# Group 0's FFN is cut in two around group 1, with second products two units behind

## The chip, the cores and the metric

The kernel runs on one core of a Trainium2 chip. The core has TensorE (PE, with its weight loads listed as PEld), VectorE (DVE), ScalarE (ACT), GpSimd (POOL) and SyncE (SP, which here only issues DMAs); each works through its own instruction list in order. The metric is device time in microseconds (us), the median of three runs.

## The reference

A linear attention runs over 768 tokens for 4 batches of 8 heads, and its output (3072 tokens by 384) goes through a feed-forward net (FFN):

```python
for t in range(768):
    cur = einsum('bhd,bhe->bhde', u * k[t], v[t])
    y[t] = einsum('bhd,bhde->bhe', r[t], state + cur)
    state = w * state + einsum('bhd,bhe->bhde', k[t], v[t])
h = x @ w_in                              # [3072,384] @ [384,2048]
out = (h * clip(h + 3, 0, 6) / 6) @ w_out # [3072,2048] @ [2048,384]
```

## The kernel before

**Attention.** Tokens are cut into 12 chunks of 64, and each chunk into two halves (two batches each): 24 halves, numbered `i`. Four halves make a group of 512 tokens, and there are six groups (`NG`). A half needs five loads at most (`load`, L199), DVE or POOL products that build `ks`, `RP`, `X` and `KH` (`prepare`, `attention`), and one block of small matmuls on PE, here called its visit (`visit`): the visit of half i adds its keys and values to the state in bank `U` (`keep`), makes its outputs (`outputs`) and, from `APART` on, also the scores of half i+1. Then DVE builds the next `X` from the scores (`choose`), DVE scales `U` into `St`, ACT copies the output to `x` as its rounded part (L404), and DVE subtracts that to get the rest (L405). After every second half six small DMAs move rows of `x` to other partitions (L412, 16 partitions each). `x` has two buffers, by group parity.

**FFN.** A unit is one group by one of 16 slices of the hidden dimension (`NF`): 96 units. `ffn1` is nine 128x512 matmuls (L137) into one of two banks `h`; ACT applies the bias and lower clip (L430), DVE clips and multiplies (L432), ACT rounds into `g` (L436), DVE subtracts to get the rest (an L196 row `g<-t,g`). `ffn2` is nine matmuls (L144) from `g` (three buffers) that add to the three PSUM banks `o`. A key `"ffn"` that all of them write keeps these blocks in the order in which they are added. After a group's slice 15 the three sums are scaled by 1/6 into SBUF, two by ACT (L460) and one by DVE (L461), and leave by DMA (L462).

**Weights.** The 64-bit weights of a slice come as one 768 KB load into one of two buffers `raw` and are converted by `weights(f)` (L212): `z` by ACT or DVE (L223), `cv` by ACT (L225) and by DVE (L226), a shift and or on DVE (L228), an add (an L196 row `z<-z,cv`), the rounded part `w_hi` by ACT or DVE (L232, L233), and the rest `w_lo` on POOL only (L234, in the trace an L196 row `w_lo<-z,w_hi`).

**Order.** Nothing is issued as written. `Schedule.add` notes each operation's cost per engine and what it reads and writes; `order` lists them with a planner: an operation's rank is the longest chain of costs behind it, each engine takes the ready operation that can begin first (by rank among those that begin within 0.1), and one that two engines could do goes to the one that would end it first. `WAIT`, `ISSUE`, `FLIGHT` and `KB_US` are the planner's prices. Where its plan leaves PE idle, filler matmuls on `ident` are put (`warm`, L532).

The loop at L497 adds units group by group. While group 0's units are added, the slices 3 to 15 are converted, one for each unit, and the attention of the next group is added at every fourth slice: `if c0 == 0 and f % 4 == 0 and 4 + 4 * g + f // 4 < NHALF: attend(4 + 4 * g + f // 4)`. So halves 4 to 7 are spread over group 0's 16 units. `ffn2` is added one unit behind: `while len(pend) > (2 if ns == 1 else 1): ffn2(*pend.pop(0))` with `ns` always 2.

Of the kernel before, what the change touches and what calls it, by code (L numbers as in the profile page):

```python
# [23 lines left out]
NHALF = 2 * NSTEP  # L24
# [14 lines left out]
WAIT = {"pe": 0.26, "act": 0.13, "dve": 0.12, "pool": 0.12, "sp": 0.05}  # L39
ISSUE, FLIGHT, KB_US = 0.46, 1.95, 300.0  # L40
LEAD = 8.0
EARLY = 8
APART = 4


class Schedule:
# [3 lines left out]
    def __init__(self):  # L50
        self.ops, self.writer, self.readers = [], {}, {}

    def add(self, costs, reads, writes, emit, lead=0.0, port=False):

        n = len(self.ops)
        deps = set()
        for r in reads:
            if r in self.writer:
                deps.add(self.writer[r])
            self.readers.setdefault(r, []).append(n)  # L60
        for w in writes:
            if w in self.writer:
                deps.add(self.writer[w])
            deps.update(self.readers.pop(w, ()))
            self.writer[w] = n
        deps.discard(n)
        self.ops.append((costs, deps, emit, lead, {"pool", "dve"} if port else {"pool"}))
        return n

    def order(self):  # L70
# [7 lines left out]
        for i in reversed(range(n)):  # L78
            costs = ops[i][0]
            w = max(WAIT[e] for e in costs)  # L80
            own = FLIGHT + costs["sp"] / KB_US if "sp" in costs else min(costs.values())
            rest[i] = own + max((rest[j] + w for j in succ[i]), default=0.0)
            rest[i] = max(rest[i], 0.0)
        prio = [rest[i] + ops[i][3] for i in range(n)]
        waits = [len(ops[i][1]) for i in range(n)]
        at = [dict.fromkeys(ops[i][0], 0.0) for i in range(n)]
        free = dict.fromkeys(WAIT, 0.0)
        port = line = 0.0
# [6 lines left out]
        while ready:  # L95
            best = None
            for e in free:
                here = [i for i in ready if e in ops[i][0]]
                if not here:
                    continue  # L100
                t = min(begin(i, e) for i in here) + 0.1
                for i in sorted((i for i in here if begin(i, e) <= t), key=lambda i: -prio[i]):
                    start = begin(i, e)
                    end = start + (ISSUE if e == "sp" else ops[i][0][e])
                    if any(begin(i, x) + c < end for x, c in ops[i][0].items() if x != e):
                        continue
                    if best is None or start < best[0]:
                        best = (start, e, i)
                    break
            start, e, i = best  # L110
            ready.remove(i)
            if e == "sp":
                free[e] = start + ISSUE
                line = ready_at = max(line, start + FLIGHT) + ops[i][0][e] / KB_US
            else:
                free[e] = ready_at = start + ops[i][0][e]
            if e in ops[i][4]:
                port = free[e]
            done.append((start, free[e], e, i))
            for j in succ[i]:  # L120
                for x in at[j]:
                    at[j][x] = max(at[j][x], ready_at + (WAIT[e] if x != e or e == "sp" else 0.03))
                waits[j] -= 1
                if not waits[j]:
                    ready.append(j)
# [14 lines left out]

def project(nc, o, w_hi, w_lo, f, g, clear, ms=range(3)):
    for m in ms:
        for k, (wl, hl) in enumerate(PARTS):
            nc.tensor.matmul(o[m], (w_hi, w_lo)[wl][:, f, 1, 128 * m:128 * m + 128], g(hl),  # L144
                             start=(clear and k == 0), stop=(f == NF - 1 and k == 2), skip_group_check=True)


def fast_path(tc, mp, pp, sb, w_hi, w_lo, b3, wm, badi, hps, ops3, rT, kT, rt, kt, vt, wp, wu, wcat, out):
# [26 lines left out]
    mask = one("mask", [128, C], U8)  # L175
    KH, ks = two("KH", [128, 8, D]), two("ks", [112, 8, C])
    NW = 2 * DM
    raw, z = two("raw", [128, NW], I64), two("z", [128, NW])
# [21 lines left out]
    def load(i):  # L200
        q = i % 2
        for name, dst, src, cost in (("kT", kTt, kT, 224), ("rT", rTt, rT, 224), ("V", V, vt, 192),
                                     ("kt", ktt, kt, 192), ("rt", rtt, rt, 192)):
            if name == "rt" and i < EARLY:
                continue
            S.add({"sp": cost}, [], [(name, q)], lambda e, dst=dst, src=src: dma(dst[q], src[i]), LEAD)
# [5 lines left out]
    def weights(f):  # L212
        S.add({"sp": 768}, [], [("raw", f % 2)], lambda e: dma(raw[f % 2], wcat[f]))
        words = "p (n two) -> p n two"
# [18 lines left out]
              else dve.tensor_copy(hi, zf), port=True)  # L233
        tensor_tensor(0.87, 1.9, [kz, ("wh", f)], [("wl", f)], lo, zf, hi.bitcast(F32), ALU.subtract, "p")  # L234


    def consts():
# [26 lines left out]

        S.add({"sp": 7}, [], ["wpt"], lambda e: dma(wpt, wp), 400)

# [109 lines left out]
    def attention(i):  # L376
# [19 lines left out]
        if going:  # L396
            S.add({"dve": 0.47}, ["U", "E"], [("St", q)], lambda e: dve.tensor_tensor(
                out=St[q], in0=U[0:112], in1=PQ[:, :, C:C + 1].broadcast_to([112, 8, D]), op=ALU.mult), LEAD)
        x = xt[g % 2]
        cs = slice(128 * hf, 128 * hf + 128)  # L400
        yt = y_[0:112].rearrange("e (p b) t -> e p b t", b=2)
        hi, lo = (x[0:112, c, :, hl, cs].rearrange("e p (b t) -> e p b t", t=C) for hl in range(2))
        kx = ("x", g % 2, c, hf)
        S.add({"act": 0.49}, [ky], [kx + (0,)], lambda e: act.copy(out=hi, in_=yt), LEAD)  # L404
        S.add({"dve": 0.60}, [ky, kx + (0,)], [kx + (1,)], lambda e: dve.tensor_tensor(  # L405
            out=lo, in0=yt, in1=hi.bitcast(F32), op=ALU.subtract), LEAD)
        if hf == 1:
            for n in range(2):
                for j in range(3):
                    r0, d0 = 64 * n + 16 * j, 64 * n + 48  # L410
                    S.add({"sp": 32}, [("x", g % 2, c, b, hl) for b in range(2) for hl in range(2)],
                          [("xh", g % 2, c, n, j)], lambda e, j=j, r0=r0, d0=d0: dma(  # L412
                              x[d0:d0 + 16, c, j].bitcast(F32), x[r0:r0 + 16, c, 3].bitcast(F32)), LEAD)
# [3 lines left out]
    def ffn1(n, g, f, c0, ns):  # L417
        x, h, t, gt = xt[g % 2], hps[n % 2], tt[n % 2], gg[n % 3]
        T = 256 * ns
# [5 lines left out]
        for c in range(c0, c0 + ns):  # L425
            reads += [("x", g % 2, c, hf, hl) for hf in range(2) for hl in range(2)]
            reads += [("xh", g % 2, c, k, j) for k in range(2) for j in range(3)]
        first = S.add({"pe": 1.03 * ns}, reads, [("h", n % 2), "ffn"], emit)
# [14 lines left out]
    def ffn2(n, g, f, c0, ns, ms=range(3)):  # L443
        T = 256 * ns
        gt = gg[n % 3]
        cols = slice(256 * c0, 256 * c0 + T)

        def emit(e):

            project(nc, [o[:, cols] for o in ops], w_hi, w_lo, f, lambda hl: gt[:, hl, :T],  # L450
                    f == 0 and c0 == 0, ms)
        S.add({"pe": 1.03 / 3 * ns * len(ms)}, [("g", n % 3, 0), ("g", n % 3, 1), ("wh", f), ("wl", f)],
              [f"o{m}" for m in ms] + ["ffn"], emit)
        if f == NF - 1:
            t0 = 512 * g + 256 * c0
            for m in ms:
                o, kb = stage[3 * c0 + m]
                o = o[:, :T]
                S.add({"act": 0.1 + 0.2 * ns} if m != 1 else {"dve": 0.05 + 0.28 * ns}, [f"o{m}"], [kb],
                      lambda e, m=m, o=o: act.mul(out=o, in_=ops[m][:, cols], mul=1.0 / 6.0) if e == "act"  # L460
                      else dve.tensor_scalar(out=o, in0=ops[m][:, cols], scalar1=1.0 / 6.0, scalar2=None, op0=ALU.mult))  # L461
                S.add({"sp": 128 * ns}, [kb], [], lambda e, m=m, o=o: dma(  # L462
                    out[128 * m:128 * m + 128, t0:t0 + T], o))

    def flag():

        wf = KH[0].rearrange("p h d -> p (h d)")[0:1]
        S.add({"sp": 2}, [], [("KH", 0)], lambda e: dma(wf, wu[0:1]))

# [11 lines left out]
    load(0)  # L481
    S.add({"sp": 192}, [], ["ubt"], lambda e: [dma(
        ubt[TOK[n]].rearrange("p h d -> p (h d)"), wu[2 + n:3 + n].broadcast_to([64, DM])) for n in range(2)])
# [5 lines left out]

    units = [(g, f, 0, 2) for g in range(NG) for f in range(NF)]  # L490
    pend, held = [], []
    for i in range(4):
        attend(i)
    for f in range(3):
        weights(f)
    nw = 3
    for n, u in enumerate(units):  # L497
        g, f, c0, ns = u
        if g == 0 and c0 == 0 and nw < NF:
            weights(nw)  # L500
            nw += 1
        if c0 == 0 and f % 4 == 0 and 4 + 4 * g + f // 4 < NHALF:
            attend(4 + 4 * g + f // 4)
        if g == NG - 2 and f == NF - 1:
            flag()
        ffn1(n, *u)
        pend.append((n,) + u)
        while len(pend) > (2 if ns == 1 else 1):
            ffn2(*pend.pop(0))
# [31 lines left out]
def rwkv_ffn_kernel(ctx: ExitStack, tc: tile.TileContext, rT, kT, rt, kt, vt, wp, wu, wcat, ys, out):  # L541
# [21 lines left out]
    with tc.If(bad != 0):  # L563
        with tc.tile_pool(name="fb", bufs=1) as fb, tc.tile_pool(name="fl", bufs=1) as fl:
# [45 lines left out]
            with tc.For_i(0, NG, 1) as g:  # L610
# [9 lines left out]
                for f in range(NF):  # L620
# [6 lines left out]
                    nc.vector.tensor_tensor(out=gt[:, 1], in0=t, in1=gt[:, 0].bitcast(F32), op=ALU.subtract)  # L627
                    project(nc, ops, w_hi, w_lo, f, lambda hl: gt[:, hl], f == 0)
                for m in range(3):
# [65 lines left out]
```

## Time and profile before

| what | value |
|---|---|
| median of three runs | 520.24 us (518.41 to 520.96) |
| the profiled execution, its own time | 523.83 us |
| its span, first to last instruction | 521.9 us |
| PE busy | 496.1 us, 95% |
| DVE busy | 302.6 us, 58% |
| ACT, POOL busy | 189.5 us (36%), 66.4 us (13%) |

The profiled execution is 3.59 us (0.7%) above the median, and 1.93 us of its time lie outside the span. Busy shares are of the whole span; matmuls are pipelined, so a busy PE may still be waiting a little or running at its lower clock. In the forty-slice view each digit is a share in tenths, 9 being 90% or more.

### The profile page before, as it was taken

How to read it: one execution, taken by the hardware profiler on the slowest of the kernel's cores; microseconds unless marked ns; L12 is line 12 of the kernel's file. 1: busy time of each engine (PE TensorE's matmuls, PEld its weight loads, DVE VectorE, ACT ScalarE, POOL GpSimd, SP SyncE). 2: the span in 40 equal slices, each digit the busy share in tenths (PEclk: the TensorE clock that was granted, in tenths of full speed). 3: DMA queues.
4: the chain of work that ended last, by engine and by line, in shares of the span. 5: the costliest groups of instructions: out<-in, count | busy, mean ns of one | idle time of the engine just before them, and what ended most of it. 6: DMA issues, size and time to landing. Idle time of an engine off the chain costs nothing.

```text
span 521.9 us, 11782 instructions
## 1 busy us (share of the span) xinstructions
PE 496.1 (95%) x5126; PEld 407.5 (78%) x5126; DVE 302.6 (58%) x469; ACT 189.5 (36%) x292; POOL 66.4 (13%) x52
## 2 busy tenths in 40 slices
PE   8868999898999999999999999999999999999994
PEld 7767787787778888778888778888788888788882
DVE  8776788887983359633379633389433372333331
ACT  2413767354333343233333333333433332333331
POOL 1411333211300011100012100023000020000000
PEclk9797999797999999999999999999999999999998
DMA  8874344553250016410026310035200010100001
GB/s 274 240 224 134 123 138 164 163 182 104 75 161 0 1 53 171 135 60 2 0 82 184 93 62 0 0 109 164 93 9 0 1 47 19 60 1 0 0 1 66
DMA packets 22908, 44.29 MB, mean 85 GB/s; under 512 B 3649, under 2 KB 11970, under 8 KB 22850
## 3 DMA queue, kind: packets, MB, share of 16 engines
q1 hardware_dynamic: 22850, 43.47, 27.3%
q8 instruction: 42, 0.69, 0.6%
q14 instruction: 16, 0.13, 0.1%
HBM read 36.38 MB, written 4.72 MB: 79 GB/s over the span
## 4 chain that ended last, share of the span: by engine, by line
PE 72%; DVE 13%; ACT 4%; issue 4%; DMA 3%; SPq 3%; POOL 0%; ACTq 0%; DVEq 0%; POOLq 0%
PE h L137 30%; PE o L144 29%; PE h L532 4%; PE Y L295 3%; PE SC L295 3%; DVE g L196 2%; SPq L412 2%; DMA kt<-kt 2%; DVE t L432 2%; DVE KH L196 1%; DMA rt<-rt 1%; PE U L295 1%; DVE x L405 1%; DVE rt L196 1%; PE o L295 1%
## 5 line engine op out<-in xcount | busy, mean ns | idle before, releaser
L144 PE MATMUL o<-g,w_hi 128*128 128x512 f32 x576 | 199.5, 400 | 3.7 <-DVE g L196 1.5
L137 PE MATMUL h<-x,w_hi 128*128 128x512 f32 x576 | 165.4, 396 | 0.0
L432 DVE SCALAR_TENSOR_TENSOR t<-t,h 128x512 f32<-128x512 f32 x96 | 65.8, 685 | 127.4 <-ACT t L430 127.4
L144 PEld LDWEIGHTS o<-g,w_hi 128*128 128x128 f32 x576 | 108.4, 189 | 33.3 <-DVE g L196 4.1
L430 ACT ACTIVATE t<-h,b 128x512 f32<-128x512 f32 x96 | 66.1, 688 | 174.4 <-PE h L137 174.2
L137 PEld LDWEIGHTS h<-x,w_hi 128*128 128x128 f32 x576 | 108.7, 190 | 23.8
L144 PE MATMUL o<-g,w_lo 128*128 128x512 f32 x288 | 113.5, 394 | 0.0
L196 DVE TENSOR_TENSOR g<-t,g 128x512 fp32r<-128x512 f32 x96 | 70.3, 732 | 45.3 <-ACT g L436 45.3
L436 ACT CAST g<-t 128x512 fp32r<-128x512 f32 x96 | 59.6, 620 | 86.7 <-DVE t L432 86.6
L137 PE MATMUL h<-x,w_lo 128*128 128x512 f32 x288 | 82.5, 395 | 0.0
L137 PEld LDWEIGHTS h<-x,w_lo 128*128 128x128 f32 x288 | 54.9, 191 | 12.3
L144 PEld LDWEIGHTS o<-g,w_lo 128*128 128x128 f32 x288 | 54.6, 189 | 11.2
L196 POOL TENSOR_TENSOR RP<-rT,E 112x512 f32<-112x512 f32 x14 | 17.2, 1228 | 234.3 <-PE Y L295 222.8
L196 POOL TENSOR_TENSOR w_lo<-z,w_hi 128x768 fp32r<-128x768 f32 x16 | 31.1, 1944 | 87.1 <-ACT w_hi L232 45.4
L295 PEld LDWEIGHTS U<-V,KH 64*48 64x48 f32 x704 | 18.7, 125 | 12.2 <-issue 9.5
L295 PE MATMUL U<-V,KH 64*48 64x48 f32 x704 | 21.6, 212 | 5.2 <-issue 3.0
L532 PEld LDWEIGHTS h<-ident 128*128 128x128 f32 x162 | 23.3, 228 | 3.2 <-DVE t L432 1.6
L295 PE MATMUL SC<-RP,ks 48*64 48x64 f32 x704 | 25.7, 224 | 0.0
L532 PE MATMUL h<-ident 128*128 128x128 f32 x162 | 24.4, 315 | 1.2 <-DVE t L432 1.2
L295 PE MATMUL Y<-X,V 64*48 64x64 f32 x704 | 25.4, 225 | 0.0
L295 PE MATMUL Y<-RP,St 48*48 48x64 f32 x672 | 23.5, 220 | 0.0
L295 PEld LDWEIGHTS SC<-RP,ks 48*64 48x64 f32 x704 | 23.0, 137 | 0.6 <-issue 0.4
(77 smaller groups left out, 357.4 us busy)
## 6 DMA issues: line engine op xcount, KB each, us to landing
raw<-wcat SPq DMA_DIRECT2D x16, 768.0 KB, 4.3
kT<-kT SPq DMA_DIRECT2D x24, 224.0 KB, 3.4
rT<-rT SPq DMA_DIRECT2D x24, 224.0 KB, 3.1
kt<-kt SPq DMA_DIRECT2D x24, 192.0 KB, 4.3
V<-vt SPq DMA_DIRECT2D x24, 192.0 KB, 4.0
rt<-rt SPq DMA_DIRECT2D x16, 192.0 KB, 4.2
outT<-cv SPq DMA_DIRECT2D x12, 256.0 KB, 2.1
x<-x SPq DMA_DIRECT2D x72, 32.0 KB, 2.0
```

The costliest lines, as they stand in the source:

```text
L137: nc.tensor.matmul(h, (w_hi, w_lo)[wl][:, f, 0, 128 * j:128 * j + 128], x(j, hl), start=(m == 0 and j == 0), stop=(m == 2 and j == 2))
L144: nc.tensor.matmul(o[m], (w_hi, w_lo)[wl][:, f, 1, 128 * m:128 * m + 128], g(hl), start=(clear and k == 0), stop=(f == NF - 1 and k == 2), ...
L196: emit = lambda e: eng[e].tensor_tensor(out=out, in0=in0, in1=in1, op=op)
L295: nc.tensor.matmul(out, lhsT, rhs, start=start, stop=True, skip_group_check=True)
L405: S.add({"dve": 0.60}, [ky, kx + (0,)], [kx + (1,)], lambda e: dve.tensor_tensor(out=lo, in0=yt, in1=hi.bitcast(F32), op=ALU.subtract), LEAD)
L412: [("xh", g % 2, c, n, j)], lambda e, j=j, r0=r0, d0=d0: dma(x[d0:d0 + 16, c, j].bitcast(F32), x[r0:r0 + 16, c, 3].bitcast(F32)), LEAD)
L430: S.add({"act": 0.13 + 0.23 * ns}, [("h", n % 2), "b3"], [kt_], lambda e: act.activation(out=t[:, :T], in_=h[:, :T], func=AF.Relu, bias=b3 ...
L432: last = S.add({"dve": 0.05 + 0.28 * ns}, [("h", n % 2), kt_], [kt_], lambda e: dve.scalar_tensor_tensor(out=t[:, :T], in0=t[:, :T], scala ...
L436: S.add({"act": 0.08 + 0.22 * ns}, [kt_], [kg + (0,)], lambda e: act.copy(out=gt[:, 0, :T], in_=t[:, :T]))
L532: nc.tensor.matmul(hps[1][:, :128], ident, ident, start=True, stop=True)
```

## The change

The order of units becomes: group 0 slices 0 to 5, all of group 1, group 0 slices 6 to 15, then groups 2 to 5. After slice 5 group 0's three sums are scaled by ACT into a new SBUF tile `part` so that the banks `o` serve group 1; at group 0's end DVE alone scales the rest and adds `part`, for all three banks. `x` buffers go by a table (`XBUF`). Halves 4 to 7 are added at units 0, 1, 3 and 4, halves 8 to 11 in group 0's second part; those of groups 3 to 5 stay at every fourth slice. Slices of weights are still added one for each of the first 13 units, which now are group 0's six and group 1's first seven. `ffn2` is added two units behind. `APART` goes from 4 to 5: half 4's scores become a visit of their own instead of a part of visit 3. `w_lo` may go to DVE as well as POOL. The planner gets start times for the engines, load costs in us, and a slack for DMA issues and POOL operations that wait on another engine.

```diff
-ISSUE, FLIGHT, KB_US = 0.46, 1.95, 300.0
+BEGIN = {"pe": 1.4, "act": 2.1, "dve": 0.9, "pool": 0.8, "sp": 0.8}
+ISSUE, FLIGHT = 0.47, 1.95
+SPARE = {"sp": 1.0, "pool": 0.8}
...
-APART = 4
+APART = 5
+SPLIT = 6
+LAG = 2
+XBUF = (0, 1, 1, 0, 1, 0)
...
+        self.ops.append((costs, deps, emit, lead, {"pool", "dve"} if port else {"pool"}, spare or self.later))
...
-        free = dict.fromkeys(WAIT, 0.0)
+        free = dict(BEGIN)
...
-                    at[j][x] = max(at[j][x], ready_at + (WAIT[e] if x != e or e == "sp" else 0.03))
+                    at[j][x] = max(at[j][x], ready_at + (WAIT[e] if x != e or e == "sp" else 0.03)
+                                   + (SPARE.get(e, 0.0) if x != e and ops[j][5] else 0.0))
...
+    part = one("part", [128, 3, 512])
...
-        tensor_tensor(0.87, 1.9, [kz, ("wh", f)], [("wl", f)], lo, zf, hi.bitcast(F32), ALU.subtract, "p")
+        tensor_tensor(0.87, 1.9, [kz, ("wh", f)], [("wl", f)], lo, zf, hi.bitcast(F32), ALU.subtract)
...
+        begins = f == 0 or (g == 0 and f == SPLIT)
+        ends = f == NF - 1 or (g == 0 and f == SPLIT - 1)
+
         def emit(e):
 
             project(nc, [o[:, cols] for o in ops], w_hi, w_lo, f, lambda hl: gt[:, hl, :T],
-                    f == 0 and c0 == 0, ms)
+                    begins and c0 == 0, ends, ms)
...
+                if g == 0:
+                    S.add({"dve": 0.05 + 0.28 * ns}, [f"o{m}", ("part", m)], [kb], lambda e, m=m, o=o:
+                          dve.scalar_tensor_tensor(out=o, in0=ops[m][:, cols], scalar=1.0 / 6.0,
+                                                   in1=part[:, m, cols], op0=ALU.mult, op1=ALU.add))
...
+        elif ends:
+            for m in ms:
+                S.add({"act": 0.1 + 0.2 * ns}, [f"o{m}"], [("part", m)], lambda e, m=m: act.mul(
+                    out=part[:, m, cols], in_=ops[m][:, cols], mul=1.0 / 6.0))
...
-    units = [(g, f, 0, 2) for g in range(NG) for f in range(NF)]
+    def group(g, fs):
+        return [(g, f, 0, 2) for f in fs]
+
+    units = group(0, range(SPLIT)) + group(1, range(NF)) + group(0, range(SPLIT, NF))
+    units += [u for g in range(2, NG) for u in group(g, range(NF))]
+    meet = {}
+    for i in range(4):
+        meet[(0, i * SPLIT // 4)] = meet.get((0, i * SPLIT // 4), []) + [4 + i]
+        at = (0, SPLIT + i * (NF - SPLIT) // 4)
+        meet[at] = meet.get(at, []) + [8 + i]
+        for g in range(2, NG - 1):
+            meet[(g, 4 * i)] = [4 + 4 * g + i]
...
+    S.later = True
     for f in range(3):
         weights(f)
...
-        if g == 0 and c0 == 0 and nw < NF:
+        if nw < NF:
...
-        while len(pend) > (2 if ns == 1 else 1):
+        while len(pend) > LAG:
             ffn2(*pend.pop(0))
```

## Rows read from the trace of the kernel before

**Rows 1.** The page: busy times, then granted clock in forty slices.

```profile
PE 496.1 (95%) x5126; PEld 407.5 (78%) x5126; DVE 302.6 (58%) x469; ACT 189.5 (36%) x292; POOL 66.4 (13%) x52
...
PEclk9797999797999999999999999999999999999998
```

**Rows 2.** PE by line, 51.3 to 149.57 (count | busy, mean).

```profile
L144 PE MATMUL o<-g,w_hi 128*128 128x512 f32 x97 | 35.1, 417 | 1.7 <-DVE g L196 0.8 <-ACT z L460 0.8
...
L137 PE MATMUL h<-x,w_hi 128*128 128x512 f32 x108 | 32.4, 412 | 0.0
```

**Rows 3.** The chain that ended last, 88 to 137 us (start, us, what).

```profile
94.57 0.48 DVE KH L196
...
99.55 3.65 PE h L137 x9
...
108.46 0.18 PE U L295 x2
...
111.15 2.27 PE o L144 x9
...
113.42 2.06 PE h L137 x9
...
117.70 1.67 issue
...
120.49 4.14 PE o L144 x9
...
124.63 2.95 PE h L137 x9
...
130.18 0.69 DVE x L405
```

**Rows 4.** By stretches: each engine busy (count), granted clock, DMA.

```profile
51.30:149.57 98.27, 91.50 (x938) 74.34 (x936) 82.89 (x118) 52.87 (x77) 25.95 (x14) 0.93 0.44 140
...
221.10:514.90 293.80, 292.23 (x2596) 237.09 (x2596) 138.95 (x217) 98.02 (x157) 19.80 (x15) 1.00 0.15 44
...
55.80:81.40 25.60, 25.52 (x109) 20.41 (x110) 22.49 (x29) 18.75 (x26) 8.94 (x5) 1.00 0.38 124
...
127.50:129.50 2.00, 2.00 (x130) 1.91 (x129) 0.66 (x2) 1.19 (x2) 0.00 (x0) 1.00 0.03 8
```

**Rows 5.** DVE by line, 44 to 81 us.

```profile
L228 DVE SCALAR_TENSOR_TENSOR z<-z,cv 128x768 int32<-128x768 int32 x7 | 9.1, 1307 | 0.0
...
L351 DVE TENSOR_TENSOR X<-idc,SC 128x512 f32<-128x512 f32 x1 | 0.7, 686 | 7.0 <-PE SC L295 7.0
```

**Rows 6.** DVE by line, 91 to 131 us.

```profile
L228 DVE SCALAR_TENSOR_TENSOR z<-z,cv 128x768 int32<-128x768 int32 x4 | 3.8, 950 | 0.0
...
L405 DVE TENSOR_TENSOR x<-Y,x 112x512 fp32r<-112x512 f32 x4 | 2.7, 676 | 0.2 <-ACT x L404 0.2
```

**Rows 7.** SP's list, 130 to 136 us (start, us, issues).

```profile
130.90 3.67 SPq L412 DMA_DIRECT2D x<-x  x6
```

**Rows 8.** The page: DMA issues (count, KB, us to landing).

```profile
x<-x SPq DMA_DIRECT2D x72, 32.0 KB, 2.0
```

**Rows 9.** The timelines of DVE and POOL, 58 to 61 us.

```profile
59.12 2.50 DVE L228 SCALAR_TENSOR_TENSOR z<-z,cv 128x768 int32<-128x768 int32 x1
...
58.96 1.85 POOL L196 TENSOR_TENSOR w_lo<-z,w_hi 128x768 fp32r<-128x768 f32 x1 [4.95 <-ACT w_hi L232]
```

**Rows 10.** Groups by line, whole span.

```profile
L461 DVE TENSOR_SCALAR cv<-o 128x512 f32<-128x512 f32 x6 | 4.1, 692 | 9.2 <-ACT cv L460 6.2 <-PE o L144 3.0
...
L460 ACT ACTIVATE z<-o 128x512 f32<-128x512 f32 x6 | 3.6, 598 | 5.7 <-DVE cv L461 5.7
```

**Rows 11.** PE's timeline at the first change of group.

```profile
149.57 0.50 PE L144 MATMUL o<-g,w_hi 128*128 128x512 f32 x1 [0.75 <-ACT z L460]
```

**Rows 12.** The chain, 505 to 523 us.

```profile
511.19 0.67 PE h L532 x6
```

**Rows 13.** The chain, 30 to 57 us.

```profile
36.16 5.58 issue
```

More of the change, by code (lines that the diff above doesn't have):

```diff
@@ L39, with add @@
 WAIT = {"pe": 0.26, "act": 0.13, "dve": 0.12, "pool": 0.12, "sp": 0.05}
-ISSUE, FLIGHT, KB_US = 0.46, 1.95, 300.0
+BEGIN = {"pe": 1.4, "act": 2.1, "dve": 0.9, "pool": 0.8, "sp": 0.8}
+ISSUE, FLIGHT = 0.47, 1.95
+SPARE = {"sp": 1.0, "pool": 0.8}
 LEAD = 8.0
 EARLY = 8
-APART = 4
+APART = 5
+SPLIT = 6
+LAG = 2
+XBUF = (0, 1, 1, 0, 1, 0)
 class Schedule:
     def __init__(self):
-        self.ops, self.writer, self.readers = [], {}, {}
-    def add(self, costs, reads, writes, emit, lead=0.0, port=False):
+        self.ops, self.writer, self.readers, self.later = [], {}, {}, False
+    def add(self, costs, reads, writes, emit, lead=0.0, port=False, spare=False):
         n = len(self.ops)
@@ L66, in add @@
         deps.discard(n)
-        self.ops.append((costs, deps, emit, lead, {"pool", "dve"} if port else {"pool"}))
+        self.ops.append((costs, deps, emit, lead, {"pool", "dve"} if port else {"pool"}, spare or self.later))
         return n
@@ L80, in order @@
             w = max(WAIT[e] for e in costs)
-            own = FLIGHT + costs["sp"] / KB_US if "sp" in costs else min(costs.values())
+            own = FLIGHT + costs["sp"] if "sp" in costs else min(costs.values())
             rest[i] = own + max((rest[j] + w for j in succ[i]), default=0.0)
@@ L113, in order @@
                 free[e] = start + ISSUE
-                line = ready_at = max(line, start + FLIGHT) + ops[i][0][e] / KB_US
+                line = ready_at = max(line, start + FLIGHT) + ops[i][0][e]
             else:
@@ L138, in hidden, with project @@
                              start=(m == 0 and j == 0), stop=(m == 2 and j == 2))
-def project(nc, o, w_hi, w_lo, f, g, clear, ms=range(3)):
+def project(nc, o, w_hi, w_lo, f, g, clear, last, ms=range(3)):
     for m in ms:
@@ L144, in project @@
             nc.tensor.matmul(o[m], (w_hi, w_lo)[wl][:, f, 1, 128 * m:128 * m + 128], g(hl),
-                             start=(clear and k == 0), stop=(f == NF - 1 and k == 2), skip_group_check=True)
+                             start=(clear and k == 0), stop=(last and k == 2), skip_group_check=True)
 def fast_path(tc, mp, pp, sb, w_hi, w_lo, b3, wm, badi, hps, ops3, rT, kT, rt, kt, vt, wp, wu, wcat, out):
@@ L201, in load @@
         q = i % 2
-        for name, dst, src, cost in (("kT", kTt, kT, 224), ("rT", rTt, rT, 224), ("V", V, vt, 192),
-                                     ("kt", ktt, kt, 192), ("rt", rtt, rt, 192)):
+        for name, dst, src, cost in (("kT", kTt, kT, 0.86), ("rT", rTt, rT, 0.86), ("V", V, vt, 0.74),
+                                     ("kt", ktt, kt, 0.74), ("rt", rtt, rt, 0.74)):
             if name == "rt" and i < EARLY:
@@ L212, in weights @@
     def weights(f):
-        S.add({"sp": 768}, [], [("raw", f % 2)], lambda e: dma(raw[f % 2], wcat[f]))
+        S.add({"sp": 2.2}, [], [("raw", f % 2)], lambda e: dma(raw[f % 2], wcat[f]))
         words = "p (n two) -> p n two"
@@ L263, in consts @@
         S.add({"pe": 2.5}, ["ident"], ["Y", "o2"], init_rows, 300)
-        S.add({"sp": 7}, [], ["wpt"], lambda e: dma(wpt, wp), 400)
+        S.add({"sp": 0.03}, [], ["wpt"], lambda e: dma(wpt, wp), 400)
         def powers(e):
@@ L398, in attention @@
                 out=St[q], in0=U[0:112], in1=PQ[:, :, C:C + 1].broadcast_to([112, 8, D]), op=ALU.mult), LEAD)
-        x = xt[g % 2]
+        x = xt[XBUF[g]]
         cs = slice(128 * hf, 128 * hf + 128)
@@ L402, in attention @@
         hi, lo = (x[0:112, c, :, hl, cs].rearrange("e p (b t) -> e p b t", t=C) for hl in range(2))
-        kx = ("x", g % 2, c, hf)
+        kx = ("x", XBUF[g], c, hf)
         S.add({"act": 0.49}, [ky], [kx + (0,)], lambda e: act.copy(out=hi, in_=yt), LEAD)
@@ L410, in attention @@
                     r0, d0 = 64 * n + 16 * j, 64 * n + 48
-                    S.add({"sp": 32}, [("x", g % 2, c, b, hl) for b in range(2) for hl in range(2)],
-                          [("xh", g % 2, c, n, j)], lambda e, j=j, r0=r0, d0=d0: dma(
+                    S.add({"sp": 0.12}, [("x", XBUF[g], c, b, hl) for b in range(2) for hl in range(2)],
+                          [("xh", XBUF[g], c, n, j)], lambda e, j=j, r0=r0, d0=d0: dma(
                               x[d0:d0 + 16, c, j].bitcast(F32), x[r0:r0 + 16, c, 3].bitcast(F32)), LEAD)
     def ffn1(n, g, f, c0, ns):
-        x, h, t, gt = xt[g % 2], hps[n % 2], tt[n % 2], gg[n % 3]
+        x, h, t, gt = xt[XBUF[g]], hps[n % 2], tt[n % 2], gg[n % 3]
         T = 256 * ns
@@ L425, in ffn1 @@
         for c in range(c0, c0 + ns):
-            reads += [("x", g % 2, c, hf, hl) for hf in range(2) for hl in range(2)]
-            reads += [("xh", g % 2, c, k, j) for k in range(2) for j in range(3)]
+            reads += [("x", XBUF[g], c, hf, hl) for hf in range(2) for hl in range(2)]
+            reads += [("xh", XBUF[g], c, k, j) for k in range(2) for j in range(3)]
         first = S.add({"pe": 1.03 * ns}, reads, [("h", n % 2), "ffn"], emit)
@@ L458, in ffn2 @@
                 o = o[:, :T]
[L459 to L462, printed above, removed]
+                if g == 0:
+                    S.add({"dve": 0.05 + 0.28 * ns}, [f"o{m}", ("part", m)], [kb], lambda e, m=m, o=o:
+                          dve.scalar_tensor_tensor(out=o, in0=ops[m][:, cols], scalar=1.0 / 6.0,
+                                                   in1=part[:, m, cols], op0=ALU.mult, op1=ALU.add))
+                else:
+                    S.add({"act": 0.1 + 0.2 * ns} if m != 1 else {"dve": 0.05 + 0.28 * ns}, [f"o{m}"], [kb],
+                          lambda e, m=m, o=o: act.mul(out=o, in_=ops[m][:, cols], mul=1.0 / 6.0) if e == "act"
+                          else dve.tensor_scalar(out=o, in0=ops[m][:, cols], scalar1=1.0 / 6.0, scalar2=None, op0=ALU.mult))
+                S.add({"sp": 0.45 * ns}, [kb], [], lambda e, m=m, o=o: dma(
                     out[128 * m:128 * m + 128, t0:t0 + T], o))
+        elif ends:
+            for m in ms:
+                S.add({"act": 0.1 + 0.2 * ns}, [f"o{m}"], [("part", m)], lambda e, m=m: act.mul(
+                    out=part[:, m, cols], in_=ops[m][:, cols], mul=1.0 / 6.0))
     def flag():
         wf = KH[0].rearrange("p h d -> p (h d)")[0:1]
-        S.add({"sp": 2}, [], [("KH", 0)], lambda e: dma(wf, wu[0:1]))
+        S.add({"sp": 0.02}, [], [("KH", 0)], lambda e: dma(wf, wu[0:1]))
         def emit(e):
@@ L481, in fast_path @@
     load(0)
-    S.add({"sp": 192}, [], ["ubt"], lambda e: [dma(
+    S.add({"sp": 0.74}, [], ["ubt"], lambda e: [dma(
         ubt[TOK[n]].rearrange("p h d -> p (h d)"), wu[2 + n:3 + n].broadcast_to([64, DM])) for n in range(2)])
@@ L498, in fast_path @@
         g, f, c0, ns = u
-        if g == 0 and c0 == 0 and nw < NF:
+        if nw < NF:
             weights(nw)
             nw += 1
-        if c0 == 0 and f % 4 == 0 and 4 + 4 * g + f // 4 < NHALF:
-            attend(4 + 4 * g + f // 4)
+        if c0 == 0:
+            for i in meet.get((g, f), ()):
+                attend(i)
         if g == NG - 2 and f == NF - 1:
@@ L627, in rwkv_ffn_kernel @@
                     nc.vector.tensor_tensor(out=gt[:, 1], in0=t, in1=gt[:, 0].bitcast(F32), op=ALU.subtract)
-                    project(nc, ops, w_hi, w_lo, f, lambda hl: gt[:, hl], f == 0)
+                    project(nc, ops, w_hi, w_lo, f, lambda hl: gt[:, hl], f == 0, f == NF - 1)
                 for m in range(3):
```

## The prediction

> **What bounds the kernel now.** I read the page first: PE is busy 95% of the span, DVE 58%, POOL 13%, and the granted clock dips only in the first quarter of the forty slices [rows 1]. So the question is not which engine is fullest but where PE's 5% and its slow stretches lie. Then the stretches: from 221.10 to 514.90 us PE is busy 292.23 of 293.80, with the clock at 1.00 (2.4 GHz) and DVE at 138.95, under half [rows 4]. There nothing but fewer matmuls would help. From 51.30 (the first FFN block) to 149.57 (the first second product of group 1) it is different: PE 91.50 of 98.27, clock 0.93, DVE 82.89 busy, 84% [rows 4].
>
> How much that stretch loses I get by counting blocks. PE's groups by line show 108 `w_hi` matmuls of L137, six in a block, so 18 first blocks, and 97 of L144, so 16 second blocks and the first matmul of the next [rows 2]. A block that nothing disturbs takes 2.06 us, such as the one at 113.42 [rows 3]. 34 blocks x 2.06 = 70.0. Four visits lie between them: the one from 108.46 to the block at 111.15 takes 2.69 [rows 3], and three are of that kind (160 records); the fourth, with 128, fits the stretch 127.50 to 129.50 and takes 2.0 [rows 4]. 3 x 2.69 + 2.0 = 10.1. So 80.1 us of work took 98.27: **18.2 us are lost in group 0**. The chain names pieces of it: a wait for no visible event of 1.67 at 117.70, then blocks of 4.14 and 2.95 in place of 2.06, before that one of 3.65 [rows 3]. TensorE was granted less than full speed there, at its lower level of 1.2 GHz in part of the stretch (mean 0.93 in [rows 4]), after PE had been stopped around visits.
>
> Why is it lost there? From 55.80 to 81.40 DVE converts about one slice for each unit and PE still runs 25.52 of 25.60 [rows 4]. In 44 to 81 us DVE did seven slices (L228 x7) and hardly any attention; in 91 to 131 us four slices, four halves' `x` (L405 x4) and attention of halves 4 to 7 [rows 5, 6]. So slices alone keep pace, slices and attention together do not; the loss begins when half 4's product `KH` comes at 94.57 [rows 3].
>
> **The change, part by part.** *The order of units.* Slices 6 to 15 are wanted six units later, attention 4 to 7 ten units earlier. So the question becomes when group 1's `x` is ready. Undisturbed, PE gets to group 1's first block after ten blocks (six first, four second products, since these now lag two units) and four visits: 51.3 + 10 x 2.06 + 10.1 = 82.0 us. Before, half 4's `KH` came at 94.57 and half 7's `x` at 130.18, 35.6 us for four halves, with four slices and about four FFN units on DVE meanwhile [rows 3, 6]. Nothing but the order on DVE parked half 4 until then: its scores were consumed at about 44 us [rows 5]. In the new order these four halves can start at 44, with slices 3 to 5 and group 0's first units beside them, much the same mix. 44 + 35.6 = 79.6; then 0.7 for the DVE operation, 3.67 for six DMA issues and 2.0 for the last to land [rows 3, 7, 8]: 86.0. One or two FFN units more than in the old mix, 1.4 of DVE each (two products of 0.69, as [rows 10] price one of that shape), make it about 88. So PE waits about **6 us** where it lost 18.2; bounds 0 (DVE hands more to POOL) and the whole 18.2.
>
> After that group 1's 16 units last 16 x 2 x 2.06 = 66 us and take ten slices, against one per unit in the stretch that PE filled [rows 4]: I take 0 for it. What hides it is that DVE's 22.49 of 25.60 is then spread over six units with no slice; without that cover it would be the old loss again. Attention 8 to 11 must now wait for group 1's last first block, since group 2 uses the same `x` buffer, and has ten units (41 us) where it had sixteen; halves 4 to 7 took 35.6 in the crowded stretch, so 0, with a bound of 3.
>
> *The extra change of group.* `part` takes three ACT operations of 0.60 [rows 10]; at group 0's end three DVE operations of 0.69 take the place of two of ACT's and one of DVE's. A first block of 2.06 lies between the last second product of one group and the first of the next, and before, PE still waited 0.75 at such a place for ACT [rows 11]. One place more, and a serial DVE at another: **+1.0**, bounds 0 and 3 x 0.69 = 2.1. The number of DMAs is unchanged; group 0's three stores go later on SP, in a stretch with little traffic.
>
> *Second products two units behind.* Between a first block and its second product lie two blocks more. At the end the fillers of 0.67 that stood in for a late `g` go [rows 12]: **-0.7**. Elsewhere after 221 us PE has 1.57 idle in all [rows 4], so no more is to be had there; in group 0 this slack is part of why I take 6 and not 10.
>
> *`w_lo` on DVE too.* DVE pays about 0.95 per slice (L228 has its size, 950 ns in [rows 6]), POOL saves 1.85 [rows 9]. But POOL's operation also stops DVE: an L228 that began 0.16 after one took 2.50 instead of 0.95 [rows 9], and in that stretch L228's mean is 1307 [rows 5]. These nearly cancel; 0, bounds -3 and +5.7 (six slices before group 1 at 0.95).
>
> *`APART`, start times, slack.* Half 4's scores leave visit 3. In visit 3 PE stood 5.58 us, waiting for no event that the profile shows [rows 13], and the first `x` of group 0, hence the start at 51.3, came after it. Visit 3 gets shorter, the new visit costs up to 1; whether the hole falls again into visit 3 I can't tell. I take 0, bounds -5.6 and +1. The slack moves DMA issues behind others in SP's list, and halves' loads behind `raw`; with prices unknown it is part of the 6.
>
> The Trainium skill ("Runtime: NRT & Kernel Launch", Instruction fetch mechanics) says that an engine fetches its next 16 KB of instructions by itself while it runs, and that crossing a block is mostly hidden. By that the hole would not be there at all; the 5.58 and 1.67 in PE's instruction-dense visits speak against it, though the trace names no cause.
>
> The Trainium skill ("SBUF — State Buffer", Who interferes with whom) says that a VectorE operation with two SBUF inputs and a GpSimd operation that reads SBUF exclude each other for the whole instruction. The 2.50 above agrees; by the rule moving `w_lo` gains, by the sum of rows it is about even.
>
> **The sum**, against the profiled execution's own 523.83: -18.2 + 6 + 1.0 - 0.7 = -11.9, so 511.9. The median is 3.59 lower; with the same term 520.24 - 11.9 = **508.3 us**.
>
> **Rivals.** *Slower: group 1 comes too late.* PE takes blocks in a fixed order, so group 1's first block stops all FFN behind it, where before only small holes arose. Gain is zero when that wait reaches 17.9, first block at 99.9, half 7's `x` at 93.5, 36.7 earlier than before. If the order keeps serving slices first as it did from 44 to 81 and the four halves then take their 35.6, half 7 comes at 116.6, 23 us past that point: 543; halfway, 530. For it: DVE is 84% busy there and slices 3 to 5 are due first. Against it: the planner ranks by the chain behind, and four halves in a row make a longer chain than a slice due at unit 12. A long stop also brings the lower clock, 2.0 for a block of 4.14. Chance 0.14.
>
> *No change:* the wait is 15 to 20 us, so DVE's work only moved. Within 2.6 of 520.24; chance 0.08.
>
> *Small gain:* the holes are PE's own and travel with the visits. Then 1.67 and the excess of the three slow blocks (1.59 + 2.08 + 0.89) remain, 6.2, beside the 6: 514.5. Both holes of the old trace lie in visits, which speaks for it. Chance 0.18.
>
> *More gain:* the 5.58 hole at the start goes and everything after it moves up: 502.7. Chance 0.15; the fetch rule above would side with it.
>
> *Forecast,* 504 to 512: 0.45. A measurement can tell about 0.5% (2.6 us) from none. Faster 0.78, same 0.08, slower 0.14. The range leaves out the slower rival and a little at the bottom: 500 to 522; without the other sign, 502 to 516.
>
> **What would show it.** Right: PE dense from the first block of group 1 to the end, clock 1.00 there; first block of group 1 at 82 to 90 us; `x` of half 7 at 76 to 84; no fillers before the last second product; one wait of about 1 us at the change of group after slice 5. Wrong: halves 4 to 7 still behind slices 6 and later in DVE's list, a PE wait over 15 us before group 1, waits for DVE inside group 1 (slices late after all), or a wait before group 2's first block (its `x` buffer free too late).

## The result, and the profile after

The changed kernel takes 512.88 us (median of four runs, 512.19 to 513.40), the kernel before 519.75 beside it (518.41 to 520.96). The ratio is 0.9867, interval 0.9839 to 0.9896: 6.9 us faster. The forecast was 508.3 (range 500 to 522): right in direction, 58% of the predicted gain, and nearest in number to the rival called small gain. Ratios and their intervals leave out a run over 1.5% above its kernel's fastest, which here is one run of e8.

The profiled execution took 512.19, its span is 510.4. The page, first the engines' busy times, then the granted clock in forty slices, answers to [rows 1]:

```profile
PE 489.8 (96%) x5068; PEld 402.5 (79%) x5068; DVE 313.3 (61%) x483; ACT 188.1 (37%) x291; POOL 46.5 (9%) x42
...
PEclk9786989999999999999999999999999999999998
```

POOL's busy time fell by 20 us and DVE's rose by 11, since `w_lo` went over; the clock still dips in the first quarter only. By stretches (as [rows 4]; first FFN block to group 1's first block, to the end of the change of group, to the last FFN block):

```profile
52.43:87.23 34.80, 31.57 (x542) 24.65 (x540) 32.10 (x46) 16.18 (x25) 7.51 (x5) 0.95 0.56 177
87.23:103.89 16.66, 14.20 (x56) 11.24 (x54) 16.56 (x20) 12.03 (x18) 4.70 (x3) 0.90 0.40 130
103.89:503.34 399.45, 398.71 (x3537) 325.26 (x3535) 220.51 (x349) 146.29 (x229) 20.65 (x16) 1.00 0.20 60
```

Read them with the prediction's prices (2.06 a block, 2.69 and 1.94 a visit; the latter is the short visit's exact length in PE's timeline). The first holds ten blocks and three visits, 27.9 us, so 6.9 are lost. Half 4's visit now comes ahead of the first FFN block, so that three visits stand behind it and not four, and the block begins 1.1 later than before. The second holds six blocks, 12.4: 4.3 lost. The third holds 176 blocks and 16 visits, 393.6: 5.9 lost. Before, 8.8 were lost over the corresponding 365.33 us from 149.57 to 514.90.

Where the first two stretches lose it, the chain shows first:

```profile
68.47 0.60 DVE t L439
69.12 3.92 PE h L143 x9
...
75.64 0.70 DVE x L412
...
79.59 0.59 SPq L419
```

A first block waits for DVE's product `t` of an earlier unit, then takes 3.92 in place of 2.06, at the lower clock in part (granted 0.83 from 66 to 76). Two more first blocks, at 77.85 and 82.97, wait 0.60 and 0.71 for a `t`. What stood ahead of these three `t` (68.40, 77.12, 82.24) is in DVE's timeline:

```profile
65.75 1.66 DVE L203 TENSOR_TENSOR w_lo<-z,w_hi 128x768 fp32r<-128x768 f32 x1
...
76.25 0.95 DVE L203 TENSOR_TENSOR w_lo<-z,w_hi 128x768 fp32r<-128x768 f32 x1
...
81.36 0.96 DVE L203 TENSOR_TENSOR w_lo<-z,w_hi 128x768 fp32r<-128x768 f32 x1
```

Twice a `w_lo`, new on DVE, is the operation just ahead of `t`; the first time a `w_lo` of 1.66 stands there, then attention's `X` and `St`. Half 7's `x` comes at 75.64, and group 1's first block at 87.23 waits for nothing.

Ahead of the first FFN block the chain has:

```profile
47.88 4.80 PE h L564 x22
52.68 2.08 PE h L143 x9
```

These are 22 fillers, in PE's timeline from 47.80 to 52.43. Group 0's last `x` DMA had landed at 46.6 (issued at 43.4, 3.2 to landing) and slice 0's `w_lo` had ended at 36.5, so PE passed 4.6 us with fillers although the trace shows nothing more for this block to wait for.

Then PE's timeline at the change of group, as [rows 11]:

```profile
96.84 0.85 PE L143 MATMUL h<-x,w_hi 128*128 128x512 f32 x3
100.15 0.80 PE L150 MATMUL o<-g,w_hi 128*128 128x512 f32 x1 [2.46 <-ACT part L481]
100.75 0.63 PE L150 MATMUL o<-g,w_lo 128*128 128x512 f32 x1
101.17 1.05 PE L150 MATMUL o<-g,w_hi 128*128 128x512 f32 x2
```

And ACT's timeline there:

```profile
93.30 0.92 ACT L230 ACTIVATE z<-raw 128x768 f32<-128x768 f32 x1 [2.57 <-DVE w_lo L203]
...
95.64 0.84 ACT L239 CAST w_hi<-z 128x768 fp32r<-128x768 f32 x1 [0.25 <-DVE z L203]
96.38 0.91 ACT L232 ACTIVATE cv<-raw 128x768 int32<-128x768 uint32 x1
97.19 0.67 ACT L437 ACTIVATE t<-h,b 128x512 f32<-128x512 f32 x1
97.76 0.89 ACT L230 ACTIVATE z<-raw 128x768 f32<-128x768 f32 x1
98.56 1.54 ACT L481 ACTIVATE part<-o 128x512 f32<-128x512 f32 x3
```

ACT's list stood 2.57 us because its `z` overwrites what `w_lo`, now on DVE, still had to read. The three scalings into `part` were ready when the second product of slice 5 ended at 95.47, but stood behind `w_hi`, `cv`, `t` and `z`. So PE waited 2.46 us and then ran at the lower clock (granted 0.55 from 100.15 to 103.89; 0.63 for a matmul that elsewhere takes 0.39).

At the end the chain has no fillers any more, against [rows 12]:

```profile
496.18 5.51 PE o L150 x24
501.69 0.02 issue
```

### The profile page after: what moved, and what is told of

The parts are those of the page before. It is cut to its first block, busy times and chain, and to the rows that moved or that the text cites. A ratio compares the mean times of both kernels' runs of the same rounds, so it can differ in the third digit from the quotient of the medians.

```text
span 510.4 us, 11667 instructions
## 1 busy us (share of the span) xinstructions
PE 489.8 (96%) x5068; PEld 402.5 (79%) x5068; DVE 313.3 (61%) x483; ACT 188.1 (37%) x291; POOL 46.5 (9%) x42
## 4 chain that ended last, share of the span: by engine, by line
PE 87%; DVE 7%; issue 2%; ACT 1%; DMA 1%; SPq 1%; POOL 0%; POOLq 0%; DVEq 0%
PE o L150 37%; PE h L143 37%; PE Y L302 5%; PE SC L302 2%; PE h L564 2%; PE U L302 2%; DMA raw<-wcat 1%; DVE RP L203 1%; PE o L302 1%; SPq L419 1%; DVE ks L203 1%; DVE z L203 1%; DVE cv L233 0%; DVE X L203 0%; DVE E L281 0%
## 5 line engine op out<-in xcount | busy, mean ns | idle before, releaser
L150 PE MATMUL o<-g,w_hi 128*128 128x512 f32 x576 | 197.0, 397 | 3.1 <-ACT part L481 2.5
L143 PEld LDWEIGHTS h<-x,w_hi 128*128 128x128 f32 x576 | 107.4, 189 | 29.0 <-DVE t L439 4.9
L203 DVE TENSOR_TENSOR g<-t,g 128x512 fp32r<-128x512 f32 x96 | 67.0, 699 | 42.0 <-ACT g L443 41.9
L150 PEld LDWEIGHTS o<-g,w_lo 128*128 128x128 f32 x288 | 54.5, 189 | 11.9
L203 POOL TENSOR_TENSOR RP<-rT,E 112x512 f32<-112x512 f32 x16 | 20.4, 1272 | 248.0 <-PE Y L302 228.0
L411 ACT CAST x<-Y 112x512 fp32r<-112x512 f32 x22 | 12.9, 586 | 43.6 <-PE Y L302 43.6
L302 PEld LDWEIGHTS U<-V,KH 64*48 64x48 f32 x704 | 19.8, 132 | 8.2 <-issue 8.1
L302 PEld LDWEIGHTS Y<-X,V 64*48 64x48 f32 x704 | 22.9, 126 | 3.2 <-issue 2.7
L302 PE MATMUL Y<-RP,St 48*48 48x64 f32 x672 | 24.6, 227 | 0.0
L302 PE MATMUL U<-V,KH 64*48 64x48 f32 x704 | 22.8, 219 | 1.1 <-issue 1.1
L302 PEld LDWEIGHTS Y<-RP,St 48*48 48x48 f32 x672 | 21.4, 127 | 0.4 <-issue 0.4
```

The source lines that it names most:

```text
L143: nc.tensor.matmul(h, (w_hi, w_lo)[wl][:, f, 0, 128 * j:128 * j + 128], x(j, hl), start=(m == 0 and j == 0), stop=(m == 2 and j == 2))
L203: emit = lambda e: eng[e].tensor_tensor(out=out, in0=in0, in1=in1, op=op)
L302: nc.tensor.matmul(out, lhsT, rhs, start=start, stop=True, skip_group_check=True)
```

## The experiments

**e1_before_again**, the kernel before with a new profile. No edit.

> The kernel before once more, unchanged, with a new profile. Theory: the profiled execution of before lost some 3.6 us more than a usual one, in holes and slow blocks of the stretch from the first FFN block to group 1's first second product. Then its own time is 519 to 521, and that stretch lasts about 94.5 us in place of 98.27, the rest being the same within 0.5. Rival: the 18.2 us are the same every time and the 3.6 lie elsewhere (start or end): the stretch is again 98 us.

Its own time was 521.46, above the 519 to 521 expected and above the 518.17 of the kernel before beside it, so this profile too may have lost more than a usual execution. By stretches:

```profile
51.18:146.01 94.83, 87.96 (x938) 71.65 (x936) 83.52 (x119) 52.87 (x77) 26.30 (x14) 0.96 0.47 147
146.01:512.40 366.39, 363.61 (x3380) 295.31 (x3380) 182.32 (x286) 121.94 (x196) 24.74 (x21) 1.00 0.17 51
```

The stretch lost 14.7, not 18.2 (94.83 against 98.27 in [rows 4]): 3.4 of the first profile's loss belong to that execution. The second stretch was 1.1 longer (366.39 against 365.33), so the whole is not explained by the first alone.

**e4_split_alone**: the new order of units, all else as before.

```diff
-APART = 5
+APART = 4
-LAG = 2
+LAG = 1
... the old prices, no start times, no slack
-ALU.subtract)
+ALU.subtract, "p")
```

> The kernel before with the new order of units alone (group 0 cut at slice six, part, the x table, the new places of attention 4 to 11); second products one unit behind, half 4 joined to visit 3, w_lo on POOL, the old prices. Theory that the order of units carries the gain: 0.985 to 0.992 of before, 512 to 516 us. Rival that the planner's prices and the two units of lag carry it: 0.997 to 1.01, the crowding of attention into six units eating what the later slices give.

506.81, ratio 0.9785 (0.9747 to 0.9823), a larger gain than the theory's 0.985 to 0.992 and than the whole change's. The order of units carries the gain; something else in the change costs time.

**e2_no_split**: the changed kernel with the groups in their old order.

```diff
-    units = group(0, range(SPLIT)) + group(1, range(NF)) + group(0, range(SPLIT, NF))
-    units += [u for g in range(2, NG) for u in group(g, range(NF))]
+    units = [u for g in range(NG) for u in group(g, range(NF))]
... attention at every fourth slice, x by parity, no part
```

> The changed kernel with groups in their natural order (no cut, no part, x by parity, attention at every fourth slice); lag of two, half 4 apart, w_lo on either engine and the new prices stay. Theory that the order carries the gain: 0.995 to 1.005 of before. Rival that lag and prices carry it: 0.985 to 0.99, the same as the changed kernel.

516.29, 0.9959 (0.9934 to 0.9984): as the theory said. Without the order the rest gives 0.4%.

**e3_lag1**: the changed kernel with `LAG = 1`.

> The changed kernel with second products one unit behind instead of two. Theory (the lag gives 0.7 at the end and a little cover in the crowded part): 513.5 to 515.5, 0.988 to 0.992 of before. Rival (the two units of lag are what lets PE run on while attention holds DVE): over 517, 0.995 or more.

514.95, 0.9923 (0.9894 to 0.9952), from 509.68 to 517.29: the median within the theory's 513.5 to 515.5, the ratio just over its 0.992; not the rival. So the lag is not what costs time.

**e5 to e8: one edit each on top of the new order alone.**

```diff
+LAG = 2                                 # e5_split_lag
+APART = 5                               # e6_split_apart
-ALU.subtract, "p")
+ALU.subtract)                           # e7_split_wlo
+BEGIN, SPARE and load costs as changed  # e8_split_prices
```

These four ran beside a kernel before of 520.44, e4 beside one of 518.17. So the medians of e4 and of these do not compare as they stand; the ratios do.

> The new order of units and second products two units behind; half 4 joined to visit 3, w_lo on POOL, the old prices. The order alone took 506.81. Theory (the lag is worth its 0.7 at the end and no more, since the order alone left PE no wait behind second products): 506.1, 504.5 to 507. Rival (the lag brings three first blocks forward, and so their slices, and gives time back): over 508.

505.63, 0.9733 (0.9687 to 0.9779): the theory.

> The new order of units with half 4's scores as a visit of their own (APART 5) and nothing else: lag one, w_lo on POOL, old prices. The order alone took 506.81. Theory that w_lo on DVE is what gives 6 us back: within 1.5 of 506.81. Rival that the visit apart does: 509 or more, with the first FFN block later than 51.15.

504.86, 0.9704 (0.9664 to 0.9745), first FFN block at 50.55: it costs nothing, rather gains.

> The new order of units with w_lo allowed on DVE and nothing else: lag one, half 4 joined, old prices. The order alone took 506.81 with all sixteen w_lo on POOL; in the changed kernel fourteen ran on DVE, which was busy 35.3 of 38.0 us before group 1. Theory that this gives the time back: 510 to 514, with PE waiting before slice 6 and DVE over 90% busy from 50 to 88 us. Rival that the prices and slack do: within 1.5 of 506.81.

507.55, 0.9765 (0.9716 to 0.9815). My theory, 510 to 514, failed: alone, `w_lo` on DVE is 0.7 over e4 by the medians and 1.0 under it by the ratios, nothing clear of noise.

> The new order of units with the planner's new start times, load costs and slack and nothing else: lag one, half 4 joined, w_lo on POOL. The order alone took 506.81. Theory that w_lo on DVE gives the time back: within 1.5 of 506.81. Rival that prices and slack do: 510 to 514.

506.66 over all six, 504.94 without the longest, 0.973 (0.9678 to 0.9782); spread from 503.81 to 513.41. The rival failed too: no single edit explains the 6 us between e4 and the change. What remained was that edits cost time together, so next the prices and `w_lo` were each taken out of the full change, and both.

**e9_wlo_pool, e10_old_prices, e11_split_lag_apart**: the changed kernel less `w_lo` on DVE, less the new prices, less both.

```diff
-ALU.subtract)
+ALU.subtract, "p")                                           # e9, e11
-BEGIN = {"pe": 1.4, "act": 2.1, "dve": 0.9, "pool": 0.8, "sp": 0.8}
+BEGIN = {"pe": 0.0, "act": 0.0, "dve": 0.0, "pool": 0.0, "sp": 0.0}
-SPARE = {"sp": 1.0, "pool": 0.8}
+SPARE = {}                                                   # e10, e11, with the old load costs
```

> The changed kernel with w_lo on POOL only; order, lag, half 4 apart and the new prices stay. The changed kernel took 512.88, the new order with lag 505.63. Theory (w_lo on DVE and the new prices cost time only together: DVE, already full before group 1, gets fourteen operations of 0.95 more): 504 to 507.5, 0.968 to 0.978 of before. Rival (prices with lag and half 4 apart make the loss): 511 to 514.

508.47, 0.9795 (0.9756 to 0.9835): between theory and rival, neither.

> The changed kernel with the old prices, no start times and no slack; order, lag, half 4 apart and w_lo on either engine stay. Theory (w_lo on DVE fills DVE whatever the prices): 507 to 511. Rival (the prices are needed for the loss): 503.5 to 506.5, 0.967 to 0.975 of before.

507.00, 0.9765 (0.9722 to 0.9809): at the theory's lower edge.

> The new order of units with lag two and half 4 apart, w_lo on POOL and the old prices: the part of the change that cost nothing in single runs. Both theories: 503 to 506, 0.967 to 0.973 of before, since lag alone gave 505.63 and half 4 apart 504.86 on top of the order. It would be wrong if the two disturb each other: over 507.

503.58, 0.9686 (0.9647 to 0.9725), as expected: the fastest of all, 9.3 us under the changed kernel. From it, the prices cost 4.9 (e9), `w_lo` on DVE 3.4 (e10), both 9.3 (the change): they add, 8.3 against 9.3, and do not need each other, against e9's theory. With lag one and half 4 joined neither had cost anything clear of noise (e7, e8). The lag is not what makes them cost: at lag one with half 4 apart, both together take 514.95 (e3, 0.9923) where e6 without them takes 504.86 (0.9704). That leaves half 4 as a visit of its own, or, with half 4 joined, that each costs only beside the other; neither was tried alone. (The changed kernel's own runs were made beside a before of 519.75, these beside 520.44.)

The time of group 1's first block and the loss at the change of group go with it roughly, both read from PE's timeline of each profile:

| kernel | median us | ratio | group 1's first block | lost at the change of group |
|---|---|---|---|---|
| e11_split_lag_apart | 503.58 | 0.9686 | 80.76 | 0.9 |
| e6_split_apart | 504.86 | 0.9704 | 83.32 | 1.0 |
| e5_split_lag | 505.63 | 0.9733 | 82.88 | 1.6 |
| e4_split_alone | 506.81 | 0.9785 | 83.93 | 1.0 |
| e10_old_prices | 507.00 | 0.9765 | 83.13 | 1.1 |
| e7_split_wlo | 507.55 | 0.9765 | 85.76 | 0.7 |
| e9_wlo_pool | 508.47 | 0.9795 | 85.74 | 1.4 |
| changed kernel | 512.88 | 0.9867 | 87.23 | 4.3 |
| e3_lag1 | 514.95 | 0.9923 | 93.56 | 1.1 |

(e8 is left out, since its profile is of its longest run. The ratios compare, as the befores differ.) Of the 9.9 us between the profiled executions of the changed kernel (512.19) and e11 (502.25), 4.8 lie ahead of the first FFN block (52.43 against 47.64), 1.7 between it and group 1's first block and 3.4 at the change of group. The first piece is of the size of the fillers there. e3 and e12 have the same 22 at that place, e9 has 1.8 us of them, e6, e10 and e11 none (e11 has 4.7 us of fillers ahead of half 4's visit, the changed kernel 2.8). No run took the fillers out, so what they cost, beside what they may keep of the clock, is not shown. Behind the change of group the five kernels with the lag lose alike, 5.5 to 5.9, so the cost of `w_lo` and the prices lies ahead of it.

In e11 the chain shows what then sets group 1's first block:

```profile
35.76 3.80 issue
...
76.08 0.60 DVE x L412
...
79.80 1.98 DMA x<-x
81.91 1.85 PE h L143 x7
```

There it is half 7's `x` and its DMAs, as the prediction had it; 76.08 against the 79.6 that I worked out. In e11's row of the table 0.8 of the 0.9 is that wait inside group 1's first block.

**e12_part_first**: ACT's list alone altered.

```diff
+    done = sorted([(began[early[i]] + 0.001, free, e, i) if i in early else (start, free, e, i)
+                   for start, free, e, i in done], key=lambda x: x[0])
... early: each scaling into part -> the second product that it reads
```

> The changed kernel with nothing but ScalarE's list altered: the three operations that scale group 0's sums into part stand ahead of the cv, t and z that stood before them, right behind the second product that they read. In the changed kernel PE waited 2.5 us for them and then ran a block at 3.74. Theory (the place in ScalarE's list makes this wait, and my +1.0 for one more change of group was 3.3 short for that reason): 509 to 510.5. Rival (DVE is full there, so the wait only moves to the next slice): 512 or more.

510.91, 0.9828 (0.9788 to 0.9867), 509.95 to 515.63: 2.0 better by the medians, short of the 510.5 that I had set as the edge and not the rival's 512, and the two ratios' intervals overlap. Its profiled execution is its longest run, so only the place is read. ACT's timeline:

```profile
102.80 1.57 ACT L481 ACTIVATE part<-o 128x512 f32<-128x512 f32 x3
104.24 0.91 ACT L232 ACTIVATE cv<-raw 128x768 int32<-128x768 uint32 x1
```

PE's timeline, the first second product of group 1:

```profile
104.42 0.50 PE L150 MATMUL o<-g,w_hi 128*128 128x512 f32 x1
```

It follows a block that began at 102.25, so 0.1 is lost where PE had waited 2.46. The place in ACT's list made that wait: shown. How much time it is worth is not.

## Why the prediction was right or wrong

*The loss lies in group 0, and the order moves it: right.* e4 alone gains 11.4 us, e2 without the order 1.9. The loss of 18.2 became 6.9 before group 1 and 4.3 at the change of group.

*Group 1's first block at about 88: the number right by luck,* 87.23. Half 7's `x` came at 75.64, just before the stated 76 to 84, and in the changed kernel the wait was not at that block: PE lost its 6.9 earlier, above all behind `t` in DVE's list. The work on the way was misjudged as well: the first FFN block came 1.1 later, and 2.7 less of visits stood behind it.

*Slices after that block for 0: right.* From 103.89 on PE is busy 398.71 of 399.45; before that, slice work is what `part` stood behind in ACT's list. *Attention 8 to 11 in ten units for 0: right,* by the same row.

*The extra change of group, +1.0: mis-sized, 4.3.* I counted the three operations' time, not what ACT's list holds ahead of them, nor the lower clock behind the wait. The serial DVE at group 0's end is the small piece: the block at 207.51 lasts 2.36, 0.30 too long.

*The lag, -0.7: mis-sized.* The loss after the crowded part fell from 8.8 (9.9 in e1) to 5.9, so 2.9 to 4.0, not all of it the lag's. Kernels that differ in the lag alone lose there 8.5 and 5.6 (e4, e5), 8.5 and 5.9 (e3, the change), 7.5 and 5.7 (e6, e11), so the lag gives 1.9 to 2.9. I counted the end alone, though [rows 11] named a wait at a change of group, which the lag covers too: in PE's timeline a later change now adds 0.14 and 0.12 to the blocks at 290.57 and 292.77.

*`w_lo` on DVE and the prices, 0 each: this step failed most.* In the setting of the change they cost 3.4 and 4.9, the second over the bound of +1 that I had set for `APART`, start times and slack together. That POOL also stops DVE, the reason for 0, holds: a `w_lo` at 91.32 took 1.95 beside a POOL `ks` from 90.94. What I missed is what a `w_lo` in DVE's list holds up: the `t` behind it, and ACT's list through the `z` buffer.

*Small gain.* Nearest in number, not in mechanism. Holes, waits for no visible event, remain, but in the changed kernel all of 0.4 us or more lie ahead of the first FFN block, and none is among the 6.9 and 4.3.

*The sum.* Against the profiled execution it was exact by luck: 523.83 - 512.19 = 11.6, forecast 11.9. The two profiles give -18.2 + 6.9 + 4.3 - 2.9, + 1.1 for the later first block, - 2.7 for the visit now ahead of it, together -11.5. So errors of +0.9, +3.3, -2.2 and -1.6 nearly cancel. The step "the median is 3.59 lower; with the same term" failed. The stretch that the change removes is also where one execution differs from the next, 18.2 in one and 14.7 in the other. The gain against a usual execution had to be smaller: of the 11.6, 4.1 is the first profile's distance to the median of before and 0.7 the new profile's to its own.

*What stays open:* how the prices (start times, load costs and slack were not parted) cost 4.9 in this setting, and how much of it is fillers. Part of the spread between profiles is PE's holes, so one profile each does not settle it.

## What to carry to other kernels

When one stage is crowded, move the work whose due time can move, and price the move by the pace that the trace shows for it; here that hit group 1's start within 1 us, in part by luck. Then try the other edits of the same change one by one and together: leaving out two that I had put at nothing gave 9.3 of the 16.9 us that e11 gains over its before (520.44). A gain that consists of removed stalls is to be set against a usual execution's stalls, not against those of the one that was profiled.

## What the runs showed of the hardware

PE stood for no event that the profile shows in every profiled execution, mostly inside visits: 5.58 before [rows 13], 3.8 in e11, 5.0, 3.6 and 2.9 in e12, whose PE, DVE, POOL and SP lists are those of the changed kernel, where the longest was 2.5. The places are not random. PE's timelines of the changed kernel, then of e12:

```profile
37.30 0.45 PE L302 MATMUL SC<-uw,X 48*64 48x1 f32 x9 [0.70 <-issue]
45.41 0.21 PE L302 MATMUL Y<-X,V 64*48 64x64 f32 x1 [2.51 <-issue]
```

```profile
39.45 0.45 PE L302 MATMUL SC<-uw,X 48*64 48x1 f32 x9 [0.49 <-issue]
48.67 0.26 PE L302 MATMUL Y<-X,V 64*48 64x64 f32 x1 [4.97 <-issue]
```

Counted in the records of PE's matmuls, the two stand behind 733 and 860 matmuls. In all fourteen profiles such waits of 1 us or more, 36 in all, come behind 223, 477, 733, 860, 1114, 1242 or 1498 matmuls (within 2), whatever stands there: behind 1114 in a first block of e12, behind 1496 in a second block of e2. These numbers lie one or two times 127 or 128 apart, so the place goes with the length of PE's list and the length of the wait does not. All lie in the first 120 us, where DMA is busiest; after 150 us, in sixteen visits of the kernel before, no such wait is longer than 0.4:

```profile
PEld U L295 <- issue: 5.1, 14, 0.4
```

(weight loads: total, times, longest). That they are instruction fetches is not shown; the even spacing speaks for something that works by stretches of the list. The prediction's sentence from the Trainium skill ("Runtime: NRT & Kernel Launch", Instruction fetch mechanics), that crossing a block of instructions is mostly hidden, agrees with the visits after 150 us; no run here shows whether the early holes are such crossings. The kernel before, 23 runs beside e1 to e4, took 515.38 to 521.21; in its two profiles the stretch from the first FFN block to group 1's first second product differs by 3.4, the one behind it by 1.1.
